# FFN2 of a retention kernel by a seven-product block scheme, in groups of two units

## The chip, the cores and the metric

The kernel runs on one core of one Trainium2 chip. The metric is the device time of one launch in microseconds, median of several runs on that core; the profile shows one such run, whose span is 1.7 to 1.9 us shorter than its time. Executions come in a fast and a slower state.

## The reference, cut to what matters

Retention (causal attention with a decay per head, no softmax) over 8 batches, 8 heads, 576 positions, 64 columns a head, and on its output `x` (4608 x 512) a feed-forward block with a squared Relu:

```python
ret = scale * (q @ k.T) * Dmat            # Dmat: gamma_h ** (i - j) for i >= j, else 0
x = (ret @ v)                             # heads side by side: 4608 x 512
h = x @ w_in                              # FFN1: 512 -> 2048
r = np.maximum(h, 0.0)
g = r * r
out = (g @ w_out).astype(np.float32)      # FFN2: 2048 -> 512
```

## The kernel before

The rows are cut into 36 units of 128. A small list scheduler in Python orders all work: each task has an engine, a key (its place), a duration as planned, the tasks it depends on and the buffers it takes; it is simulated once, and the instructions of each engine are issued in that order. So the order on an engine is fixed when the kernel is built, and an instruction that waits holds up what stands behind it on its engine.

Most units go in groups of 4, so that FFN1's moving operand is 512 wide. ScalarE takes the Relu out of the accumulating bank, VectorE squares it, and FFN2 runs per unit with 16 matmuls of N=512 (`NF` is 16 blocks of the hidden layer, `NP` 4 of the model width `DM` = 512, `P` is 128):

```python
sizes = [1, 1, 2, 2, 2] + [4] * 7
...
nc.tensor.matmul(tile_of["ph", g, fb][:, j, :], lhsT=w_in16[:, m, fi * P:(fi + 1) * P],
                 rhs=tile_of["x", us[0]][:, m, :], start=(m == 0), stop=(m == NP - 1))      # FFN1, L559
...
nc.scalar.activation(out=t, in_=tile_of["ph", g, fb], func=ACTF.Relu)                       # rl, L567
...
nc.vector.tensor_tensor(out=t, in0=rl, in1=rl, op=ALU.mult)                                 # gT, L572
...
nc.tensor.matmul(tile_of["po", u, lo], lhsT=tile_of["g", g, fi // nf][:, fi % nf, s * P:(s + 1) * P],
                 rhs=w_out16[:, fi, lo:hi], start=(fi == 0), stop=(fi == NF - 1))           # FFN2, L589
...
nc.scalar.copy(out=o, in_=tile_of["po", u, lo])                                             # to SBUF, then stored
```

GpSimd feeds the retention part. For each unit it casts k twice and q once from fp32 to fp16 (one input each) and multiplies v with a column of decays; it reads all four from SBUF. In what follows these four are "the casts of a unit". The cast k and q then go through DMA transposes, out of a few staging buffers `kq`.

Of the kernel before, what the change touches and what calls it, by code (L numbers as in the profile page):

```python
# [101 lines left out]
def kernel(  # L102
# [9 lines left out]
    nc = tc.nc  # L112
# [16 lines left out]

    sizes = [1, 1, 2, 2, 2] + [4] * 7  # L130
    assert sum(sizes) == NU
    groups = []
    for n in sizes:
        first = sum(len(g) for g in groups)
        groups.append(list(range(first, first + n)))
    groups[-1][-2:] = groups[-1][:-3:-1]
    group_of = {u: g for g, us in enumerate(groups) for u in us}
# [5 lines left out]
    work = ctx.enter_context(tc.tile_pool(name="work", bufs=3))  # L143
    o_pool = ctx.enter_context(tc.tile_pool(name="o", bufs=3))
    x_pool = ctx.enter_context(tc.tile_pool(name="x", bufs=3))
    st_pool = ctx.enter_context(tc.tile_pool(name="st", bufs=5))
    g_pool = ctx.enter_context(tc.tile_pool(name="g", bufs=32))
    r_pool = ctx.enter_context(tc.tile_pool(name="r", bufs=3))
    ps_ff = ctx.enter_context(tc.tile_pool(name="ps_ff", bufs=3, space=bass.MemoryType.PSUM))
    ps_sc = ctx.enter_context(tc.tile_pool(name="ps_sc", bufs=2, space=bass.MemoryType.PSUM))  # L150
# [46 lines left out]
    for hp in range(NP):  # L197
        nc.scalar.activation(out=gam_f[:, hp, :], in_=iota_f, func=ACTF.Exp, scale=lncol[:, hp:hp + 1])
    gam = {"full": gam_f}
    dec128 = const.tile([P, NP], FP32, name="dec128")  # L200
# [4 lines left out]
    vps = [const.tile([P, NP, 192], FP16, name=f"vp{i}") for i in range(NB)]  # L205
    NT = 3
    kTs = [const.tile([P, NP, 2, P], FP16, name=f"kTb{i}") for i in range(NT)]

# [6 lines left out]

    NK = 3
    kqs = [const.tile([P, 3 * NP, P], FP16, name=f"kq{i}") for i in range(NK)]
# [3 lines left out]
    for t in kqs[1:]:  # L221
# [3 lines left out]
    L = 2 * NF  # L225
    WARM = 48
    XBAR = 8
    FIRST = ["u0", "u1", "u2", "u3", "w0", "w1", "w2", "w3", "w4", "w5", "w6", "w7"]
    sched = Schedule(dict(ff=3, psc=2, psT=1, psS=1, psO=1, ld=5, wst=4, k16=4, q16=2,
                          qT=3, rT=2, x=3, rl=3, o=3, R=5, kqT=3))  # L230
    add = sched.add
# [37 lines left out]
    def make_tail_pool():  # L269
        make_mask("tail")  # L270
        nc.gpsimd.memset(mask["tail"][0:64, 64:128], 0.0)
        iota_pt = tile_of["iota_pt"] = const.tile([P, 1], FP32, name="iota_pt")
        nc.gpsimd.tensor_copy(out=iota_pt[0:64], in_=iota_p[0:64])
        nc.gpsimd.tensor_scalar(out=iota_pt[64:128], in0=iota_p[64:128], scalar1=-64.0, scalar2=None, op0=ALU.add)
        gam_t = gam["tail"] = const.tile([P, NP, P], FP32, name="gam_tail")
        nc.gpsimd.tensor_copy(out=gam_t[:, :, 0:64], in_=gam_f[:, :, 0:64])
        nc.gpsimd.tensor_copy(out=gam_t[:, :, 64:128], in_=gam_f[:, :, 0:64])
    tail_pool = add_gated("POOL", 4, "v", 2.2, make_tail_pool)
# [57 lines left out]
    def add_ret(u):  # L336
        kind, b, c = units[u]
        us = groups[group_of[u]]
        base = (u - len(us)) * L
        early = u < ahead  # L340
# [43 lines left out]
        def ft(i, src):  # L384
            def f():
                if i == 0:
                    tile_of["psk", u] = ps_one.tile([P, 2, NP, P], FP16, name="psT", tag="psT")
                elif early:
                    tile_of["psq", u] = ps_sc.tile([P, 2, NP, P], FP16, name="psTq", tag="psc")
                else:  # L390
                    tile_of["psq", u] = tile_of["psk", u]
                for hp in range(NP):
                    nc.tensor.transpose(tile_of["ps" + src[0], u][:, i, hp, :],  # L393
                                        tile_of[src, u][:, hp * P:(hp + 1) * P], ident)
            return f
# [17 lines left out]
        else:  # L413
            prev = [T["score", u - NT]] if u >= NT else zeroed[u]
            tk = add("PE", base - 17.6, 0.22, ft(0, "k16"), deps=[ck] if early else [ck, cq], acq=("psT",))
            tq = add("PE", base - 17.5, 0.22, ft(1, "q16"), deps=[cq, tk], acq=("psc",) if early else ())
# [5 lines left out]
            if early:  # L422
                sched.free("psT", [e0, e1])
                sched.free("psc", [eq])
            else:
                sched.free("psT", [e0, e1, eq])
            transposed = [e0, e1, eq]
# [8 lines left out]
        if kind == "full":  # L436
# [15 lines left out]
            else:  # L452
                def fr0():
                    tmp = tile_of["tmp", u] = work.tile([P, NP, P], FP32, name="stmp", tag="stmp", bufs=2)
                    nc.vector.tensor_tensor(out=tmp, in0=tile_of["psS", u].rearrange("p n a d -> p n (a d)"),  # L455
# [72 lines left out]
        def fx():  # L528
            if s == 0:
                tile_of["x", us[0]] = x_pool.tile([P, NP, len(us) * P], FP16, name="xT", tag="xT")  # L530
            nc.vector.tensor_tensor(out=tile_of["x", us[0]][:, :, s * P:(s + 1) * P], in0=tile_of["psO", u],  # L531
                                    in1=gam[kind], op=ALU.mult)
        T["x", u] = add("DVE", base + 22.6, 0.7, fx, deps=[outs[-1]] + ([T["x", us[0]]] if s else []),
                        acq=() if s else ("x",))
        sched.free("psO", [T["x", u]])
        T["out", u] = outs[-1]


    T["ff2"] = []

    def add_ff(g):
# [5 lines left out]
        sq = []  # L547
        done = g - 1
        while done >= 0 and sum(4 * len(groups[i]) for i in range(done, g + 1)) <= 32:
            done -= 1  # L550
        before = [T["ff2"][done]] if done >= 0 else []
        for fb in range(NF // nf):
            for j in range(nf):
                def f(fb=fb, j=j):
# [3 lines left out]
                    for m in range(NP):  # L558
                        nc.tensor.matmul(tile_of["ph", g, fb][:, j, :], lhsT=w_in16[:, m, fi * P:(fi + 1) * P],  # L559
                                         rhs=tile_of["x", us[0]][:, m, :], start=(m == 0), stop=(m == NP - 1))  # L560
                f1.append(add("PE", base + (nf * fb + j) * n, 0.01 + 0.2133 * n, f,
                              deps=[T["x", u] for u in us] + before + wcast[(nf * fb + j) // 4] + f1[-1:],
                              acq=("ff",) if j == 0 else ()))
# [4 lines left out]

            def fg(fb=fb):
                t = tile_of["g", g, fb] = g_pool.tile([P, nf, n * P], FP16, name="gT", tag="gT")  # L570
                rl = tile_of["rl", g, fb]
                nc.vector.tensor_tensor(out=t, in0=rl, in1=rl, op=ALU.mult)  # L572
            r = add("ACT", base + 4 * fb + 4, 0.6, fr, deps=[f1[-1]], acq=("rl",))
            sched.free("ff", [r])
            sq.append(add("DVE", base + 4 * fb + 6, 0.45, fg, deps=[r]))
            sched.free("rl", [sq[-1]])
        sched.free("x", [f1[-1]])
        for s, u in enumerate(us):
            kind, b, c = units[u]
            end = base + NF * (n + s + 1)  # L580
            f2 = T["ff2"][-1:] if s == 0 else f2[-1:]

            cuts = [(0, DM)] if u != groups[-1][-1] else [(0, DM // 2), (DM // 2, DM)]
            for ci, (lo, hi) in enumerate(cuts):
                for fi in range(NF):
                    def f(fi=fi, s=s, u=u, lo=lo, hi=hi):
                        if fi == 0:
                            tile_of["po", u, lo] = ps_ff.tile([P, hi - lo], FP32, name="po", tag="ff")
                        nc.tensor.matmul(tile_of["po", u, lo], lhsT=tile_of["g", g, fi // nf][:, fi % nf, s * P:(s + 1) * P],  # L589
                                         rhs=w_out16[:, fi, lo:hi], start=(fi == 0), stop=(fi == NF - 1))  # L590
                    f2.append(add("PE", base + NF * (n + s) + fi / len(cuts) + 8 * ci, 0.0025 + 0.2135 / len(cuts), f,
                                  deps=[sq[fi // nf]] + wcast[4 + fi // 4] + f2[-1:],
                                  acq=("ff",) if fi == 0 else ()))

                def fo(u=u, lo=lo, hi=hi):
                    o = tile_of["o", u, lo] = o_pool.tile([P, hi - lo], FP32, name="o", tag="o")
                    nc.scalar.copy(out=o, in_=tile_of["po", u, lo])  # L597

                def fd(u=u, kind=kind, b=b, c=c, lo=lo, hi=hi):
                    o = tile_of["o", u, lo]  # L600
                    if kind == "full":
                        r0 = b * S + c * P
                        nc.scalar.dma_start(out=out[r0:r0 + P, lo:hi], in_=o)
                    else:
                        for i in range(2):
                            r0 = (b + i) * S + 512
                            nc.scalar.dma_start(out=out[r0:r0 + 64, :], in_=o[i * 64:(i + 1) * 64])
                oc = add("ACT", end + 1, 0.12 + 0.47 / len(cuts), fo, deps=[f2[-1]], acq=("o",))
                sched.free("ff", [oc])
                st = add("ACT", end + 1.1, 0.05, fd, deps=[oc], after=2.5)  # L610
                sched.free("o", [st])
        T["ff2"].append(f2[-1])

# [38 lines left out]
```

## Time and profile before

| | before |
|---|---|
| time, median of 3 runs | 323.06 us (322.87 to 323.6) |
| span of the profiled run | 322.6 us (this run took 324.27) |
| matmuls of FFN1 and FFN2 | 1008 of N=512, 224 of N=256 |
| FFN2 of two units | 32 matmuls of N=512 x 0.2158 = 6.9 us |
| VectorE, ScalarE, GpSimd busy | 57%, 40%, 36% |

The prediction below shows the lines that this rests on. They are to be read so: TensorE issues without a gap from about 72 us on, so the only measure of its work is the distance from one matmul's start to the next one's (0.2158 us at N=512, 0.1090 at N=256, 0.0557 at N=128). From this I work out two numbers of every trace. "Steps" is the sum of these distances over all matmuls, by their widths. A "stall" is what the distance between two consecutive starts has beyond the step of the first. Before has 308.5 us of steps and 7.4 us of stalls, nearly all ahead of 72 us.

### The profile page before, as it was taken

Reading aid. Unit: us, or ns where it says so; the run is one execution under the profiler, and the core shown is the slowest. Engines: PE = TensorE matmul, PEld = TensorE weight load, DVE = VectorE, ACT = ScalarE, POOL = GpSimd, SP = SyncE. Lnnn points to the kernel's source line nnn. Section 1 sums busy time; section 2 is a strip of 40 time slices with the busy share of each in tenths; the row PEclk is TensorE's granted clock in tenths of the full one; section 3 lists DMA queues with packets and bytes.
Section 4 is the critical chain, followed back from the end, with each engine's and each line's share of the span. In section 5 each row is a group of like instructions: output and inputs, shape, how many; then the busy total and the mean of one; then the engine's idle time right before and its main releaser. Section 6 shows DMA issues by size and latency. Waiting matters only on the chain.

```text
span 322.6 us, 5955 instructions
## 1 busy us (share of the span) xinstructions
PE 312.5 (97%) x2304; PEld 182.1 (56%) x2304; DVE 183.9 (57%) x341; ACT 128.8 (40%) x217; POOL 115.7 (36%) x167
## 2 busy tenths in 40 slices
PE   5999989989999999999999999999999999999996
PEld 2679746766855555555555555555555555554444
DVE  3496528676947843863488447833685367523500
ACT  4448843522515511551155115511552155215611
POOL 5724486625535643343347433323334200000000
PEclk9999999999999999999999999999999999999999
DMA  9999999999999999999999987799323802010012
GB/s 169 218 375 385 345 231 235 215 199 216 230 213 214 202 196 266 227 213 242 245 227 228 197 221 165 141 193 209 73 50 83 163 33 51 33 67 33 0 65 69
DMA packets 166061, 57.55 MB, mean 178 GB/s; under 512 B 157200, under 2 KB 157456, under 8 KB 166032
## 3 DMA queue, kind: packets, MB, share of 16 engines
q1 hardware_dynamic: 160640, 47.72, 74.2%
q10 hardware_dynamic: 5392, 9.44, 8.8%
q8 instruction: 18, 0.29, 0.4%
q14 instruction: 11, 0.09, 0.1%
HBM read 36.70 MB, written 9.44 MB: 143 GB/s over the span
## 4 chain that ended last, share of the span: by engine, by line
PE 85%; DMA 7%; DVE 4%; issue 1%; POOL 1%; ACT 1%; POOLq 0%; SPq 0%
PE po L589 36%; PE ph L559 33%; PE psO L512 4%; PE psc L480 4%; PE warm L242 3%; DMA wo<-in_moe_w_out_dram 3%; PE psS L441 2%; DMA kqT<-kq 2%; PE psO L516 2%; DMA out_dram<-o 1%; DVE rT L488 1%; DMA k<-in_k_dram 1%; DVE R L460 1%; DVE stmp L455 1%; PE psT L393 0%
## 5 line engine op out<-in xcount | busy, mean ns | idle before, releaser
L589 PE MATMUL po<-w_out,gT 128*128 128x512 f16 (+1 forms) x592 | 144.5, 373 | 1.0 <-POOL w_out L321 1.0
L559 PE MATMUL ph<-xT,w_in 128*128 128x512 f16 (+2 forms) x768 | 138.0, 326 | 0.0
L567 ACT ACTIVATE rl<-ph 128x512 f16<-128x512 f32 x144 | 85.6, 597 | 58.3 <-PE ph L559 54.4
L559 PEld LDWEIGHTS <-w_in 128*128 128x128 f16 x768 | 66.7, 98 | 42.0
L572 DVE TENSOR_TENSOR gT<-rl 128x512 f16<-128x512 f16 x144 | 71.7, 511 | 28.6 <-ACT rl L567 27.7
L589 PEld LDWEIGHTS <-gT 128*128 128x128 f16 x592 | 55.8, 98 | 45.5 <-issue 1.2
L597 ACT COPY o<-po 128x512 f32<-128x512 f32 (+1 forms) x37 | 21.2, 574 | 115.6 <-PE po L589 101.7
L365 POOL TENSOR_TENSOR vp<-v,vdec_full 128x512 f16<-128x512 f32 x32 | 34.0, 1064 | 38.8 <-PE psO L516 17.4
L488 DVE TENSOR_TENSOR rT<-psc,mask_full 128x512 f16<-128x512 f32 x64 | 41.6, 681 | 4.7 <-PE psc L480 4.4
L531 DVE TENSOR_TENSOR xT<-psO,gam_full 128x512 f16<-128x512 f32 x32 | 22.1, 690 | 34.6 <-PE psO L516 23.0
L512 PEld LDWEIGHTS <-vp 128*128 128x128 f16 x288 | 25.4, 98 | 15.9 <-issue 1.0
L348 POOL CAST kq<-k 128x512 f16<-128x512 f32 x28 | 19.2, 684 | 42.3 <-DMA kqT<-kq 21.4
L512 PE MATMUL psO<-rT,vp 128*128 128x128 f16 x288 | 34.0, 219 | 0.2
L455 DVE TENSOR_TENSOR stmp<-psS,R 128x512 f32<-128x512 f32 x24 | 16.5, 689 | 25.0 <-PE psS L441 24.7
L356 POOL CAST kq<-q 128x512 f16<-128x512 f32 x28 | 19.5, 696 | 28.9 <-DMA kqT<-kq 23.0
L480 PEld LDWEIGHTS <-kqT 128*128 128x128 f16 x224 | 19.3, 98 | 16.0 <-DMA kqT<-kq 2.3
L480 PE MATMUL psc<-kqT 128*128 128x128 f16 x224 | 26.1, 219 | 1.9 <-DMA kqT<-kq 1.9
L352 POOL CAST k<-k 128x512 f16<-128x512 f32 x36 | 23.3, 647 | 8.3 <-PE psS L441 5.6
L460 DVE TENSOR_TENSOR R<-stmp,bdec 128x512 f16<-128x512 f32 x24 | 18.4, 765 | 0.8
L242 PE MATMUL warm<-kq,ident 128*128 128x512 f16 x48 | 15.5, 438 | 3.3 <-DVE kq L218 3.3
L516 PE MATMUL psO<-kqT,R 128*128 128x128 f16 (+1 forms) x104 | 17.9, 211 | 0.0
L441 PEld LDWEIGHTS <-k 128*128 128x128 f16 x128 | 9.8, 98 | 6.2
(63 smaller groups left out, 123.0 us busy)
## 6 DMA issues: line engine op xcount, KB each, us to landing
k<-in_k_dram SPq DMA_DIRECT2D x32, 256.0 KB, 4.8
q<-in_q_dram SPq DMA_DIRECT2D x32, 256.0 KB, 5.0
v<-in_v_dram SPq DMA_DIRECT2D x32, 256.0 KB, 5.0
out_dram<-o ACTq DMA_DIRECT2D x31, 256.0 KB, 3.7
wi<-in_moe_w_in_dram SPq DMA_DIRECT2D x4, 1024.0 KB, 10.5
wo<-in_moe_w_out_dram SPq DMA_DIRECT2D x4, 1024.0 KB, 9.3
out_dram<-o ACTq DMA_DIRECT2D x10, 128.0 KB, 2.4
k<-in_k_dram SPq DMA_DIRECT2D x8, 128.0 KB, 5.0
```

What stands on the lines that cost most here:

```text
L242: nc.tensor.matmul(warm_ps[0], lhsT=ident, rhs=junk, start=True, stop=True)
L352: nc.gpsimd.tensor_copy(out=t, in_=tile_of["k32", u].rearrange("p h d -> p (h d)"))
L365: nc.gpsimd.tensor_tensor(out=vo, in0=tile_of["v32", u].rearrange("p (n a) d -> p n a d", a=2), in1=vdec[kind].rearrange("p (n a o) -> p n ...
L480: nc.tensor.matmul(tile_of["psc", u, half][:, j, a, :], lhsT=k_T(hp, a), rhs=q_T(hp), start=True, stop=True)
L488: nc.vector.tensor_tensor(out=tile_of["rT", u][:, 2 * half:2 * half + 2].rearrange("p n a i -> p (n a) i"), in0=tile_of["psc", u, half].re ...
L512: nc.tensor.matmul(ps[:, hp, :], lhsT=vps[u % NB][:, hp, a * 64:a * 64 + P], rhs=tile_of["rT", u][:, hp, a, :], start=(a == 0), stop=(a == ...
L516: nc.tensor.matmul(ps[:, hp, lo:hi], lhsT=tile_of["R", ru][:, hp, :], rhs=q_T(hp)[:, lo:hi], start=False, stop=(n == len(inter) - 1))
L531: nc.vector.tensor_tensor(out=tile_of["x", us[0]][:, :, s * P:(s + 1) * P], in0=tile_of["psO", u], in1=gam[kind], op=ALU.mult)
L559: nc.tensor.matmul(tile_of["ph", g, fb][:, j, :], lhsT=w_in16[:, m, fi * P:(fi + 1) * P], rhs=tile_of["x", us[0]][:, m, :], start=(m == 0) ...
L567: nc.scalar.activation(out=t, in_=tile_of["ph", g, fb], func=ACTF.Relu)
L572: nc.vector.tensor_tensor(out=t, in0=rl, in1=rl, op=ALU.mult)
L589: nc.tensor.matmul(tile_of["po", u, lo], lhsT=tile_of["g", g, fi // nf][:, fi % nf, s * P:(s + 1) * P], rhs=w_out16[:, fi, lo:hi], start=( ...
```

## The change

The intent is to take matmul columns off TensorE. For two units A and B, FFN2 is a product of a 2x2 block matrix G (rows: units A, B; columns: the halves of the hidden layer) with a 2x2 block matrix W. The change computes it with seven block products in place of eight (Strassen's scheme in its variant with few sums). The sums of W's blocks (`wT`) are made once; the sums of G's blocks (S1 to S4, each in two halves, so eight operations of 128x512 a group) are made on VectorE for every group. Partial sums that two results need are read out of the bank, after which the next product is added to the same bank. All FFN groups become groups of two, five of the eight squares of a group move to ScalarE, and retention runs 20 places further ahead. The diff, cut to its core:

```diff
-    sizes = [1, 1, 2, 2, 2] + [4] * 7
+    sizes = [1, 1] + [2] * 17
...
-    NK = 3                                  # staging buffers of the DMA transposes
+    NK = 2
...
+    EARLY = 20
+    SQ_ACT = (0, 2, 3, 5, 7)
...
-        base = (u - len(us)) * L
+        base = (u - len(us)) * L - EARLY
...
+    t1 = add_wT(0, wB[0, 1], wB[0, 0])      # wB: blocks of w_out; wT: their differences, once
+    t2 = add_wT(1, wB[1, 1], wT[0])
+    t3 = add_wT(2, wB[1, 1], wB[0, 1])
+    t4 = add_wT(3, wB[1, 0], wT[1])
...
+                if on_act:
+                    nc.scalar.activation(out=t, in_=rl, func=ACTF.Square)
+                else:
+                    nc.vector.tensor_tensor(out=t, in0=rl, in1=rl, op=ALU.mult)
...
+    # G(s, i, h): unit s, hidden half i, half h of it;  Sx(k, h): half h of sum k   (VectorE, L665)
+        s3 = add_sum(2, base - 12, G(0, 0, h) - G(1, 0, h), needs low squares)
+        s1 = add_sum(0, base,      G(1, 0, h) + G(1, 1, h), needs all squares)
+        s2 = add_sum(1, base + 1,  Sx(0, h) - G(0, 0, h),   needs s1[h])
+        s4 = add_sum(3, base + 4,  G(0, 1, h) - Sx(1, h),   needs s2[h])     # written short
...
+                    for i in (2 * q, 2 * q + 1):
+                        nc.tensor.matmul(tile_of["pb", g, bank], lhsT=left(i), rhs=right[:, i, :],
+                                         start=(start and i == 0), stop=(i == HF - 1), skip_group_check=not start)
...
+        p1 = product(1, 0, "a", raw(0, 0), wB[0, 0], low, True, True, [])
+        c1 = on_act_copy("p1", "a", 5, [p1])                 # reads the bank, which goes on adding
+        p7 = product(7, 4, "c", summed(2), wT[2], lambda h: [s3[h]], True, True, [])
+        p6 = product(6, 8, "a", summed(1), wT[1], lambda h: [s2[h]], False, True, [c1])
+        c2 = on_act_copy("u2", "a", 13, [p6])
+        p2 = product(2, 12, "b", raw(0, 1), wB[1, 0], high, True, True, [])
+        d11 = on_dve_add(uA, 0, "b", "p1", 17, [p2, c1], ("o",))
+        p5 = product(5, 16, "a", summed(0), wT[0], lambda h: [s1[h]], False, True, [c2])
+        c4 = on_act_copy("u4", "a", 21, [p5])
+        d22 = on_dve_add(uB, 1, "c", "u4", 22, [p7, c4], ("o",))
+        p3 = product(3, 20, "a", summed(3), wB[1, 1], lambda h: [s4[h]], False, True, [c4])
+        p4 = product(4, 24, "c", raw(1, 1), wT[3], high, False, True, [d22])
```

The left operand of product 6 is S2 = S1 - G of A's first half, and S1 needs the last square of the group. So between the last block of FFN1 and the second half of product 6 lies a chain on ScalarE and VectorE: Relu, square, S1, S2. TensorE covers it with retention work, product 1 and product 7. In the views below `gT<-rl` is a square, `gS<-gT` a half of S3 or S1, `gS<-gS,gT` a half of S2, and `gS<-gT,gS` a half of S4.

## The prediction

> **What bounds the kernel now.** I read the page's busy table and slices first, then the chain that ended last, then the costliest groups, and last the order in time of TensorE, VectorE and ScalarE in the steady part.
>
> ```profile
> span 322.6 us, 5955 instructions
> ...
> PE 312.5 (97%) x2304; PEld 182.1 (56%) x2304; DVE 183.9 (57%) x341; ACT 128.8 (40%) x217; POOL 115.7 (36%) x167
> ...
> PE   5999989989999999999999999999999999999996
> ...
> PEclk9999999999999999999999999999999999999999
> ...
> PE 85%; DMA 7%; DVE 4%; issue 1%; POOL 1%; ACT 1%; POOLq 0%; SPq 0%
> ...
> L572 DVE TENSOR_TENSOR gT<-rl 128x512 f16<-128x512 f16 x144 | 71.7, 511 | 28.6 <-ACT rl L567 27.7
> ```
>
> TensorE is busy 97%, and the chain of waits is 85% TensorE. But a busy TensorE need not be a full one, since the ends of matmuls are modelled. So I take starts, not durations, from the chain of waits in order of time (start, us, what):
>
> ```profile
> 81.79 2.18 PE ph L559 x20
> ...
> 291.67 13.81 PE ph L559 x64
> ```
>
> 20 matmuls of N=256 (group of two) step by 2.18/20 = 0.1090 us; 64 of N=512 step by 13.81/64 = 0.2158 us; N=128 steps by 0.0557 (8 scores in 0.45). One group of four units in the steady part, from its first hidden-layer matmul at 128.11 to the next group's at 160.66, lasts 32.55 us. Its work is 64+64 matmuls of N=512 (27.62), about 84 of N=128 (4.68) and 8 of N=64 (0.2): 32.5 us. There is no idle time in it. TensorE is the bound by issue rate itself, from about 72 us on. Idle TensorE exists only before that: 0.98 us on the w_out cast, then 1.41 and 0.47 us on transposed k and q:
>
> ```profile
> 65.11 0.62 PE L480 MATMUL psc<-kqT 128*128 128x128 f16 x8 [1.41 <-DMA kqT<-kq]
> ...
> 70.35 0.29 PE L480 MATMUL psc<-kqT 128*128 128x128 f16 x2 [0.47 <-DMA kqT<-kq]
> ```
>
> Columns taken off TensorE therefore come off the time, as long as VectorE and ScalarE can bear what is put on them. These lines say how fast VectorE is (start, us, operation, count):
>
> ```profile
> 132.27 2.60 DVE L572 TENSOR_TENSOR gT<-rl 128x512 f16<-128x512 f16 x4
> 134.83 0.69 DVE L531 TENSOR_TENSOR xT<-psO,gam_full 128x512 f16<-128x512 f32 x1
> ...
> 262.89 1.22 DVE L572 TENSOR_TENSOR gT<-rl 128x512 f16<-128x512 f16 x3
> ...
> 269.60 0.42 DVE L572 TENSOR_TENSOR gT<-rl 128x512 f16<-128x512 f16 x1
> ```
>
> An fp16 product in SBUF takes 0.42 us alone, but 0.65 each in the run at 132.27, when GpSimd was casting. The mean of all is 0.511. An operation reading PSUM takes 0.69, with a step of about 0.61 when the next one follows at once. ScalarE's Relu takes 0.60, a copy of 128x256 0.37.
>
> **What the Trainium skill says.** "TensorE: Matmul & The Clock Gate", section Back-to-back issue gap, gives N/2.4 + 2.5 ns: 109 for N=256 and 216 for N=512. The trace agrees (109.0, 215.8). So two halves cost 1% more than one whole. The same section's other figure, about 131 ns for N=512 in a stream with weight loads, is contradicted by the 215.8, which has a load per matmul. "VectorE: DVE Perf Modes", The perf-mode tier table: tensor_tensor reaches 2x with 16-bit SBUF operands, 1x with any PSUM operand. 0.42 against 0.69 agrees, so the new sums should be of the fast kind. "SBUF — State Buffer", Who interferes with whom: a VectorE instruction with two SBUF inputs contends with a GpSimd one that reads SBUF. The 0.42 against 0.65 agrees. Every new sum has two SBUF inputs. "PSUM — Partial Sum Buffer", The four PSUM rules: a matmul without the first flag adds to what stands in the bank. Nothing in this trace shows a bank read halfway and then added to; before, each bank is read once after its last matmul.
>
> **The change part by part.** There are 19 groups now: two of 1, seventeen of 2. Fifteen (units 4 to 33) use Strassen; the last is ordinary.
>
> 1. FFN2. Per Strassen group, 32 matmuls of N=512 (6.906 us) become 7 products of 8, 56 of N=256 (6.104): -0.802, times 15 = -12.0 us.
> 2. FFN1. 28 units go from groups of 4 to groups of 2: per four units 64 x 0.2158 = 13.81 becomes 128 x 0.1090 = 13.95: +0.14, times 7 = +1.0 us. Counted the other way from the built order: 1008 matmuls of N=512 and 224 of N=256 become 80 and 1960: 241.9 us becomes 230.9. TensorE's sum: -11.0 us.
> 3. VectorE, per Strassen group: 5 of 8 squares leave for ScalarE (-5 x 0.51); 8 half sums of 128x512 fp16 come (+8 x 0.51 = 4.1) and 3 additions of PSUM and SBUF, 128x256, which I estimate at 0.69 less 256 elements at 0.96 GHz = 0.42 each (1.3). Net +2.8, times 15 = 42 us. Once, 8 sums of weight blocks of 1024 elements, at about 0.7 each: 5.5. VectorE goes from 184 to about 231 of some 313, 74%.
> 4. ScalarE: +5 squares (0.60, as Relu, same width and no second table load in the order), 2 copies of 0.585 become 4 of 0.37: +3.3 per group, 50 in all: 129 becomes 179, 57%.
> 5. GpSimd only loses the tail gamma tile. DMA bytes are unchanged. Retention runs 20 keys, 20/32 of a unit, further ahead of its group; q and k staging buffers fall from 3 to 2.
>
> **The steady period by hand.** Per group TensorE needs 64 x 0.109 + 56 x 0.109 + 2 x 1.27 (retention) = 15.6 us, against 16.3 for two units before. I walk the built order with the durations above, time zero being the end of FFN1's second block. The eighth block ends at 5.8. ScalarE after it: relus 2 to 8 and squares of blocks 3, 4, 6, 8, eleven operations of 0.6 in all counting relu 2, end at about 7.2, 1.45 after the eighth block. TensorE meanwhile has 6 matmuls of retention, product 1 with 6 more (done at +1.55), product 7 (+2.42), then product 6, whose second half comes at +2.85. Product 1's copy out of its bank (0.37) ends at about +2.1; product 6, which adds to that bank, is to start at +2.42: 0.3 to spare. Product 6's second half needs a VectorE chain of 14 operations from the square of the second block (start 0.97) on: 3 squares and 7 sums at a step of 0.435 (0.511 less the overlap of 0.08), two PSUM masks, stmp and R, 2.6 together, and 0.45 for four dependent pairs. That is 7.4, so done at 8.35, or +2.6: 0.25 to spare. With sums at the contended 0.65, six of ten, it would be late by about 1 us. After that come product 2, product 5, the next group's first block, product 3, and product 4; their additions and copies have some 0.3 us or more each. ScalarE's last store issue waits for the last addition and ends 0.4 before the next relu.
>
> So the order fits, with small spare at two places. I take 0.2 us of stalls per group on average, 3 us over 15. The two early waits on transposed k and q should go, as units 8 and 9 are scored later relative to their load (-1.9), but the weight sums load VectorE in 42 to 58 us, where it had 7 us free of 16 (+1). The end is unchanged: last outputs still in two halves; the last group's FFN1 without retention beside it has ScalarE 11 x 0.6 = 6.6 against TensorE's 6.1, hidden because FFN2 needs the last square only 3 us later.
>
> Sum: 323.1 - 11.0 - 1.9 + 1.0 + 3.0 = 314.2; I choose 313.8, since the contention falls when GpSimd ends.
>
> **The rivals.** First, VectorE becomes the bound. For it: 14 us of busy time per 15.6 us period (3 squares, 8 sums, 3 additions, 4 masks, 2 x, 2 stmp, 2 R), strict order on the engine, and contention on ten operations of the critical chain. Against it: busy durations overlap by 0.08 each when operations follow at once, so it needs about 12.2. If it is true, each group stalls 0.8 us or more, the gain is eaten, and the time is 322 or worse. Second, the shared bank: read, wait, add again, three times a group; each round trip is matmul end, semaphore, 0.37 us copy, semaphore. The order puts another product (0.87) between, so it is hidden, unless ScalarE is late: its 7.8 us of FFN1 work barely fits the 7.6 of TensorE's. If exposed at 0.3 us a time, 13 us are lost and the result is within 2%. Third, a supply limit: two staging buffers instead of three for the DMA transposes (4.7 us each, one per 7.8 us). In the kernel before GpSimd waited up to 7.1 us for these buffers without TensorE ever waiting after 71 us; five units of buffering remain, so I give it little. It would show as TensorE waiting for kqT, some us.
>
> **Range and chances.** With no stall at all and the early waits gone: 310.2. With 0.5 us per group: 318. I take 310.5 to 318.5. The limit of 2% is 316.6, which needs stalls of about 0.38 us per group. Faster 0.82, same 0.16, slower 0.02.
>
> **What will show it.** The step of 56 product matmuls near 0.109; TensorE's busy near 301 to 304; VectorE 225 to 235, ScalarE near 179; sums near 0.5 us and 0.42 after GpSimd ends; the period of a Strassen group 15.6 to 15.9. If TensorE waits for gS, VectorE was too slow; if for copies of po, the bank trip is exposed; if for kqT, supply. A step of product matmuls clearly over 0.109, or sums at 1x (0.65 or more alone), would break the prediction.

## The result

| | before | changed kernel |
|---|---|---|
| time, median | 322.97 us (322.87 to 323.6, 4 runs) | 318.92 us (318.02 to 319.73, 4 runs) |
| span of the profiled run | 322.6 us | 317.0 us |
| TensorE: steps + stalls | 308.5 + 7.4 | 297.4 + 12.9 |
| VectorE, ScalarE busy | 183.9, 128.8 us | 226.3, 176.8 us |

The ratio is 0.987, with a 95% interval of 0.984 to 0.990. Ratios here are the mean time of one kernel's fast runs over that of the other's in the same rounds, so they aren't quite the ratios of the medians quoted. A gain of 4 us came where 9 were predicted. The result was computed right.

The page of the changed kernel (span; TensorE in 40 slices; the chain that ended last, by engine):

```profile
span 317.0 us, 7736 instructions
...
PE   5999979999999999999999999999999998999995
...
PE 67%; DVE 14%; DMA 8%; SPq 5%; issue 3%; ACT 2%; POOL 1%; ACTq 0%; DVEq 0%
```

In the chain TensorE falls from 85% to 67% and VectorE rises from 4% to 14%: the end is now in part set by VectorE, although TensorE's slices look as full as before. The waits of the changed kernel say where (engine, line, waited for: us in total, times, longest):

```profile
POOL kq L350 <- DMA kqT<-kq: 61.7, 16, 8.8
...
DVE gS L665 <- ACT gT L612: 4.6, 16, 0.4
...
PE po L687 <- DVE gS L665: 5.1, 7, 1.1
```

TensorE waits 7 times for a half sum `gS`, 5.1 us by the view. Counted from starts it is 7.0 us ahead of the products that read half sums, all of it product 6's second half waiting for S2, in 9 of 15 groups. Waits for copies of the bank don't appear: product 1's copy ends 2.12 us after FFN1's last block, and product 6 starts at 2.42. The groups of VectorE operations (us busy, mean ns):

```profile
L614 DVE TENSOR_TENSOR gT<-rl 128x512 f16<-128x512 f16 x64 | 31.7, 495 | 25.9 <-ACT rl L602 25.5
L665 DVE TENSOR_TENSOR gS<-gT 128x512 f16<-128x512 f16 x60 | 29.4, 489 | 5.8 <-ACT gT L612 4.6
...
L665 DVE TENSOR_TENSOR gS<-gT,gS 128x512 f16<-128x512 f16 x30 | 17.6, 586 | 0.0
L665 DVE TENSOR_TENSOR gS<-gS,gT 128x512 f16<-128x512 f16 x30 | 16.4, 546 | 1.0
L710 DVE TENSOR_TENSOR o<-po,u 128x256 f32<-128x256 f32 x30 | 12.6, 419 | 22.9 <-PE po L687 22.1 <-ACT u L700 0.8
```

These means are close to what was predicted (0.511 for a sum, 0.42 for an addition out of PSUM). The means hide two kinds of groups. First a stalled one. VectorE in order of time (start, us, operation), FFN1's last block ending at 162.91:

```profile
163.12 0.42 DVE L665 TENSOR_TENSOR gS<-gS,gT 128x512 f16<-128x512 f16 x1
163.46 0.83 DVE L614 TENSOR_TENSOR gT<-rl 128x512 f16<-128x512 f16 x1
164.21 0.83 DVE L665 TENSOR_TENSOR gS<-gT,gS 128x512 f16<-128x512 f16 x1
164.96 0.83 DVE L665 TENSOR_TENSOR gS<-gT 128x512 f16<-128x512 f16 x1
165.82 1.15 DVE L665 TENSOR_TENSOR gS<-gS,gT 128x512 f16<-128x512 f16 x1
```

GpSimd in the same stretch of the same trace:

```profile
163.14 0.87 POOL L350 CAST kq<-k 128x512 f16<-128x512 f32 x1 [7.11 <-issue]
163.96 0.81 POOL L354 CAST k<-k 128x512 f16<-128x512 f32 x1
164.71 0.80 POOL L358 CAST kq<-q 128x512 f16<-128x512 f32 x1
165.48 1.21 POOL L367 TENSOR_TENSOR vp<-v,vdec_full 128x512 f16<-128x512 f32 x1
```

TensorE, at the first and second half of product 6:

```profile
164.45 1.47 PE L687 MATMUL po<-wT,gS 128*128 128x256 f16 x12
167.02 0.61 PE L687 MATMUL po<-wT,gS 128*128 128x256 f16 x4 [1.10 <-DVE gS L665]
```

While TensorE stands there, product 2 stands behind product 6, though it reads only squares, and the last of these was done at 164.37.

The two engines take turns. Each VectorE operation ends 0.28 us after a cast ends, and the next one 0.27 us or so after the next cast. A sum that takes 0.42 alone takes 0.83, the cast beside it 0.80 in place of the 0.61 of most casts in this trace, and both go on at one pair per 0.75 us, where VectorE alone goes on at 0.34. Beside the multiply of v a sum takes 1.15. S2's second half ends at 166.97, where an undisturbed group (2.38 us after FFN1) would have had it at 165.29, and TensorE stands for 1.3 us (1.10 by the view, which counts from a modelled end).

An undisturbed VectorE stretch in the group before (FFN1's last block ends at 147.34) has its casts 0.8 us later:

```profile
147.89 0.42 DVE L614 TENSOR_TENSOR gT<-rl 128x512 f16<-128x512 f16 x1
148.22 0.42 DVE L665 TENSOR_TENSOR gS<-gT,gS 128x512 f16<-128x512 f16 x1
148.83 0.56 DVE L665 TENSOR_TENSOR gS<-gT 128x512 f16<-128x512 f16 x1 [0.19 <-ACT gT L612]
149.42 0.72 DVE L665 TENSOR_TENSOR gS<-gS,gT 128x512 f16<-128x512 f16 x1
150.06 0.68 DVE L534 TENSOR_TENSOR xT<-psO,gam_full 128x512 f16<-128x512 f32 x1
```

GpSimd there:

```profile
148.34 0.78 POOL L350 CAST kq<-k 128x512 f16<-128x512 f32 x1 [6.47 <-DMA kqT<-kq]
149.06 0.81 POOL L354 CAST k<-k 128x512 f16<-128x512 f32 x1
149.81 0.80 POOL L358 CAST kq<-q 128x512 f16<-128x512 f32 x1
150.58 1.04 POOL L367 TENSOR_TENSOR vp<-v,vdec_full 128x512 f16<-128x512 f32 x1
```

Only two chain operations are touched, S2 ends 2.80 us after FFN1, and TensorE, which comes to it at 2.86, doesn't wait. The `xT` at 150.06, which has only one input in SBUF, takes its usual 0.68 beside two of the casts.

So the theory after reading the trace (theory 1): GpSimd's reading casts and VectorE's two-input operations take turns at one place, and a group stalls when a unit's casts fall on the chain. Its rivals: VectorE simply has too much to do in the chain (theory 2, the prediction's first rival), or the order of work on VectorE puts other operations ahead of S2 (theory 3).

### The profile page after: what moved, and what is told of

Read it like the earlier page. It is cut to its first block, busy times and chain, and to the rows that moved or that the text cites. A ratio compares the mean times of both kernels' runs of the same rounds, so it can differ in the third digit from the quotient of the medians.

```text
span 317.0 us, 7736 instructions
## 1 busy us (share of the span) xinstructions
PE 302.6 (95%) x3112; PEld 260.3 (82%) x3112; DVE 226.3 (71%) x433; ACT 176.8 (56%) x327; POOL 118.9 (38%) x163
## 4 chain that ended last, share of the span: by engine, by line
PE 67%; DVE 14%; DMA 8%; SPq 5%; issue 3%; ACT 2%; POOL 1%; ACTq 0%; DVEq 0%
PE ph L594 28%; PE po L687 23%; DVE gS L665 8%; PE po L635 6%; DMA wi<-in_moe_w_in_dram 4%; PE psc L482 4%; SPq L298 4%; DMA wo<-in_moe_w_out_dram 3%; PE psO L514 3%; DVE gT L614 3%; DVE rT L490 2%; PE psS L443 2%; PE psO L518 1%; ACT rl L602 1%; ACT gT L612 1%
## 5 line engine op out<-in xcount | busy, mean ns | idle before, releaser
L594 PE MATMUL ph<-xT,w_in 128*128 128x256 f16 (+1 forms) x1216 | 140.2, 267 | 0.5 <-POOL w_in L323 0.5
L594 PEld LDWEIGHTS <-w_in 128*128 128x128 f16 x1216 | 109.9, 98 | 11.8 <-POOL w_in L323 0.7
L350 POOL CAST kq<-k 128x512 f16<-128x512 f32 x28 | 18.9, 674 | 99.1 <-DMA kqT<-kq 61.7
L687 PEld LDWEIGHTS <-gS 128*128 128x128 f16 x480 | 44.9, 98 | 12.6 <-DVE gS L665 7.9
L687 PE MATMUL po<-wT,gS 128*128 128x256 f16 x360 | 48.9, 273 | 5.4 <-DVE gS L665 5.1
L612 ACT ACTIVATE gT<-rl 128x512 f16<-128x512 f16 x80 | 50.4, 630 | 2.6
L614 DVE TENSOR_TENSOR gT<-rl 128x512 f16<-128x512 f16 x64 | 31.7, 495 | 25.9 <-ACT rl L602 25.5
L700 ACT COPY u<-po 128x256 f32<-128x256 f32 x30 | 11.2, 373 | 53.9 <-PE po L687 53.9
L687 PE MATMUL po<-w_out,gT 128*128 128x256 f16 x240 | 37.6, 273 | 0.0
L687 PEld LDWEIGHTS <-gT 128*128 128x128 f16 x360 | 32.3, 98 | 2.7 <-issue 0.2
L665 DVE TENSOR_TENSOR gS<-gT 128x512 f16<-128x512 f16 x60 | 29.4, 489 | 5.8 <-ACT gT L612 4.6
L635 PE MATMUL po<-w_out,gT 128*128 128x512 f16 (+1 forms) x112 | 23.5, 349 | 1.8 <-POOL w_out L323 1.8
```

The costliest lines, as they stand in the source:

```text
L612: nc.scalar.activation(out=t, in_=rl, func=ACTF.Square)
L635: nc.tensor.matmul(tile_of["po", u, lo], lhsT=tile_of["g", g][:, fi, s * P:(s + 1) * P], rhs=w_out16[:, fi, lo:hi], start=(fi == 0), stop= ...
L665: nc.vector.tensor_tensor(out=Sx(k, h), in0=in0(h), in1=in1(h), op=op)
L687: nc.tensor.matmul(tile_of["pb", g, bank], lhsT=left(i), rhs=right[:, i, :], start=(start and i == 0), stop=(i == HF - 1), skip_group_chec ...
```

## The experiments

All are timed against the kernel before on the same chip. The last column takes the stalls ahead of the half-sum products out of the profiled run's own time.

| run | median us | ratio [95%] | these stalls, us | profiled time less these stalls |
|---|---|---|---|---|
| changed kernel | 318.92 | 0.987 [0.984, 0.990] | 7.0 | 311.7 |
| changed kernel again | 317.94 | 0.983 [0.980, 0.985] | 6.4 | 311.8 |
| pool_gated | 312.32 | 0.968 [0.965, 0.970] | 0.2 | 311.8 |
| pool_writes (wrong result) | 313.07 | 0.969 [0.966, 0.972] | 0.1 | 313.7 |
| pool_collide | 329.70 | 1.021 [1.018, 1.025] | 18.8 | 311.1 |
| s2_first | 315.92 | 0.979 [0.977, 0.981] | 4.8 | 311.7 |
| both | 313.18 | 0.970 [0.968, 0.972] | 0.8 | 312.0 |
| gated_sq_dve | 313.80 | 0.972 [0.970, 0.974] | 1.1 | 312.9 |
| early0 | 317.66 | 0.985 [0.982, 0.987] | 6.2 | 312.6 |
| gated_early0 | 313.38 | 0.970 [0.968, 0.972] | 1.0 | 313.0 |
| nk3 | 316.48 | 0.979 [0.976, 0.982] | 4.3 | 311.3 |
| no_strassen | 323.55 | 1.002 [1.000, 1.005] | none | 323.6 |
| before again (one look) | 322.78 | | none | 322.8 |

The eleven runs with the seven products differ by 17 us in their medians, and without this one stall their profiled runs lie within 2.6 us of each other.

### Is it GpSimd? Casts held back until S2 is done (pool_gated)

One element of the finished second half of S2 is copied by GpSimd, and the casts of the units that come next are put behind that copy:

```diff
+        def fgate():
+            t = tile_of["gate", g] = work.tile([P, 1], FP16, name="gate", tag="gate", bufs=2)
+            nc.gpsimd.tensor_copy(out=t, in_=Sx(1, 1)[:, HF // 2 - 1, P - 1:P])
+        gt = add("POOL", -6 * L, 0.1, fgate, deps=[s2[1]])
+        for w in (uA + 6, uB + 6):
+            for x in T.get(("burst", w), []):      # tasks: k's two casts, q's cast, v's product
+                sched.need(x, gt)
```

> Right result. In each Strassen group GpSimd may begin the casts of two later units only after it has read one element of the last half of sum S2, so its casts cannot fall on the VectorE chain that ends with S2. Theory A (the lost gain is TensorE waiting for S2 because GpSimd reads and two-input VectorE operations take turns): the stalls ahead of product 6's second half, 7.0 us in the changed kernel's trace, fall below 1.5 us, sums in the chain take 0.42 to 0.45 us, time about 312.5 to 314. Theory B (VectorE has simply too much work per group, whoever else runs): stalls stay at 6 us or more, time 318 to 319. Theory C (supply: casts delayed by the gate come too late): stalls move to TensorE waiting for transposed k and q or for vp, time 319 or more.

It ran in 312.32 us, 6.6 below the changed kernel, with a right result. Page (span, TensorE in slices, chain):

```profile
span 310.3 us, 7730 instructions
...
PE   5989979999999999999999999999999999999995
...
PE 85%; DMA 8%; SPq 5%; POOL 1%; issue 0%; ACT 0%
```

VectorE is gone from the chain. Its operations in order of time, one group (FFN1's last block ends at 160.51):

```profile
161.06 0.42 DVE L615 TENSOR_TENSOR gT<-rl 128x512 f16<-128x512 f16 x1
161.40 0.42 DVE L666 TENSOR_TENSOR gS<-gT,gS 128x512 f16<-128x512 f16 x1
162.00 0.42 DVE L666 TENSOR_TENSOR gS<-gT 128x512 f16<-128x512 f16 x1 [0.19 <-ACT gT L613]
162.46 0.43 DVE L666 TENSOR_TENSOR gS<-gS,gT 128x512 f16<-128x512 f16 x1
...
165.17 1.38 DVE L463 TENSOR_TENSOR R<-stmp,bdec 128x512 f16<-128x512 f32 x1
```

The chain now runs at 0.42. The turn-taking isn't gone: it fell on the retention state `R`, another operation with two SBUF inputs (mean 0.88 here, 0.78 in the changed kernel), where it costs little: in the five groups in which `R` took 1.37 to 1.38 us, and in no other, product 4 started 0.16 us late (it waits for an addition that VectorE does after `R`), 0.8 us in the whole run. Steady periods are 15.56 to 15.94 us; in the changed kernel they reach 17.05.

### Is it the reading, or the time at which GpSimd works? (pool_writes)

From unit 8 on, GpSimd does five memsets per unit in place of the casts and the multiply, so it writes no less than before and reads nothing (it is busy for 101.2 us, against 118.9). The result is wrong.

```diff
+            if xbar:
+                nc.gpsimd.memset(
+                    kq[:, 0:2 * NP].rearrange("p (n a) (b d) -> p n (a b) d", a=2, d=64)[:, :, 0:4:3, :], 0.125)
+                nc.gpsimd.memset(t, 0.125)
+                return
...
+                nc.gpsimd.memset(kq[:, 2 * NP:].rearrange("p n c -> p (n c)"), 0.125)
...
+                nc.gpsimd.memset(vo, 0.125)
+                nc.gpsimd.memset(vo, 0.125)
```

> Wrong result on purpose. From unit 8 on, GpSimd writes constants of the same shapes (5 memsets per unit in place of 3 casts and a product) and reads nothing. If it is GpSimd's reading that slows the two-input VectorE operations, the sums take 0.42 us throughout although GpSimd is as busy as before, stalls ahead of product 6 fall below 1 us, time 312 to 314. If any GpSimd work slows them, sums stay near 0.49 to 0.59 mean and time 317 to 319.

313.07 us; one of its four runs was slow (319.53 at a granted clock of 0.989) and isn't in the ratio. The median of the three fast ones is 312.37. The same group as the stalled one above (FFN1's last block ends at 162.41), GpSimd:

```profile
162.29 0.52 POOL L351 MEMSET kq<- 128x512 f16 x1 [3.57 <-DMA kqT<-kq]
162.76 0.52 POOL L353 MEMSET k<- 128x512 f16 x1
163.22 0.52 POOL L359 MEMSET kq<- 128x512 f16 x1
163.69 0.52 POOL L368 MEMSET vp<- 128x512 f16 x1
```

VectorE in the same stretch:

```profile
162.96 0.42 DVE L618 TENSOR_TENSOR gT<-rl 128x512 f16<-128x512 f16 x1
163.29 0.42 DVE L669 TENSOR_TENSOR gS<-gT,gS 128x512 f16<-128x512 f16 x1
163.90 0.43 DVE L669 TENSOR_TENSOR gS<-gT 128x512 f16<-128x512 f16 x1 [0.19 <-ACT gT L616]
164.36 0.42 DVE L669 TENSOR_TENSOR gS<-gS,gT 128x512 f16<-128x512 f16 x1
```

GpSimd is as near as can be in time, and VectorE isn't touched. So it is neither GpSimd's being at work nor its writing; what the casts and the product have beyond a memset is that they read (and convert or multiply what they read; no run parts these two). The Trainium skill says this in "SBUF — State Buffer", Who interferes with whom (a VectorE instruction with two SBUF inputs contends with a GpSimd instruction that reads SBUF, not with one that only writes), and both halves of the sentence are seen here: 0.83 beside reads, 0.42 beside writes. In its fast runs it is as fast as pool_gated (312.37 and 312.32). The profiled run is the slowest of the three, and has an early wait of 1.9 us for a transposed k and q.

### Casts put on the chain on purpose (pool_collide)

The same gate, reading S3, which is done about 0.95 us ahead of FFN1's end:

```diff
-            nc.gpsimd.tensor_copy(out=t, in_=Sx(1, 1)[:, HF // 2 - 1, P - 1:P])
-        gt = add("POOL", -6 * L, 0.1, fgate, deps=[s2[1]])
+            nc.gpsimd.tensor_copy(out=t, in_=Sx(2, 1)[:, HF // 2 - 1, P - 1:P])
+        gt = add("POOL", -6 * L, 0.1, fgate, deps=[s3[1]])
```

> Right result. The same gate read as in the gated kernel, but on the last half of sum S3, which is done about 0.95 us before the end of FFN1: GpSimd's casts then begin just ahead of the S1 and S2 chain in all 13 groups that have later units, not in some. Theory A: each of those groups shows the stall of 0.85 to 1.0 us that the changed kernel shows where its casts began at -1.3 to -0.9 us, so stalls ahead of product 6 of 11 to 13 us, time 322 to 325, the whole gain gone. Rival: the gate itself gained (GpSimd's casts in pairs, less waiting on its buffers): then it gains wherever it stands, and the time stays at 312 to 314.

329.70 us, 17.4 slower than with the gate that reads S2, and 4.7 above the range expected. The waits, and two groups of VectorE operations of it:

```profile
PE po L696 <- DVE gS L666: 16.5, 13, 1.8
```

```profile
L666 DVE TENSOR_TENSOR gS<-gT,gS 128x512 f16<-128x512 f16 x30 | 29.8, 992 | 0.0
...
L666 DVE TENSOR_TENSOR gS<-gS,gT 128x512 f16<-128x512 f16 x30 | 19.6, 654 | 1.0
```

The S4 sums, of which the first half stands in VectorE's order ahead of the second halves of S1 and S2, take 0.99 us on average, against 0.47 in pool_gated, and the S2 sums 0.65 against 0.43. The groups stall by up to 1.9 us. The expectation was too low because two units' casts now follow each other: while the first unit's four are being worked off the chain falls behind, and then it meets the second unit's (in the group whose FFN1 ends at 149.47 the first four run from 148.83 to 152.12 and the next begin at 152.19; S2 ends at 153.90, 4.4 us after FFN1).

### Is it the load, or the order, on VectorE? (s2_first, both, gated_sq_dve)

s2_first puts S1 and S2 ahead of S4 and of the next `xT`, which takes operations out of the chain (theory 3). "both" does this and has the gate.

```diff
-        s4 = add_sum(..., lambda h: [s2[h]])
+        s4 = add_sum(..., lambda h: [s2[h], s2[1]])
+        if uB + 2 < NU:
+            sched.need(T["x", uB + 2], s2[1])
```

> Right result. Only VectorE's order: both halves of S1 and S2 go ahead of S4 and of the evacuation xT, which product 6 does not need. Theory A or B (the chain that ends with S2 is too long): one contended sum (0.83 us) less ahead of S2, so each stalled group gets 0.5 to 0.8 us back, stalls 7.0 to about 2, time 313.5 to 315.5. If the late product is not due to the chain's length but to ScalarE's last square: no change, 318 to 319.

> Right result. The gate after S2 together with VectorE's order S1, S2 ahead of S4 and xT. With no contention left on the chain the order has nothing to win: the stalls of product 6 are already 0.2 us in the gated kernel. Expected the same as the gated kernel within 0.3%, 311.5 to 313.5; a time below 311 would say that the chain still costs something that the stalls do not show.

s2_first ran in 315.92 us, about halfway and 0.4 above the range expected: 4.8 us of stalls remain where about 2 were expected, because a sum beside the multiply of v is as slow in the new order. VectorE and GpSimd in one group of it:

```profile
196.45 0.64 DVE L665 TENSOR_TENSOR gS<-gT 128x512 f16<-128x512 f16 x1
197.13 1.15 DVE L665 TENSOR_TENSOR gS<-gS,gT 128x512 f16<-128x512 f16 x1
```

```profile
196.02 0.80 POOL L358 CAST kq<-q 128x512 f16<-128x512 f32 x1
196.78 1.21 POOL L367 TENSOR_TENSOR vp<-v,vdec_full 128x512 f16<-128x512 f32 x1
```

"both" took 313.18 us, 0.9 more than the gate alone. A shorter chain is worth nothing once the casts are off it, and putting the sums first makes others wait: TensorE's stalls ahead of the retention products that read masked scores (`psO<-rT,vp`) are 1.6 us in place of 0.1.

The sharpest test of theory 2 loads VectorE more: the gate, with all eight squares back on VectorE.

```diff
-    SQ_ACT = (0, 2, 3, 5, 7)
+    SQ_ACT = ()
```

> The gated version, with all eight squares of a group back on VectorE (none on ScalarE); the kernel's own scheduler orders the work anew. VectorE then gets five more operations of 0.42 us per group, a step of 0.34 each, so about 1.7 us more in a period of 15.6; ScalarE loses 5 x 0.63. Theory A (what cost the change its time is GpSimd's turn-taking, not VectorE's load): the load still fits, the group's last square even ends sooner, since ScalarE does only relus; stalls ahead of the products from half sums stay under 0.3 us per group and the time is 311 to 315. Theory B (rival 1 as predicted: VectorE as such is too full for its chain): 1.7 us more in the chain shows as 0.8 us or more of stall per group, and the time is 322 or more.

313.80 us. Its page (busy times; chain):

```profile
PE 302.7 (97%) x3112; PEld 261.1 (84%) x3112; DVE 257.7 (83%) x513; ACT 133.7 (43%) x247; POOL 120.3 (39%) x178
...
PE 83%; DVE 7%; DMA 5%; issue 2%; ACT 1%; POOL 1%; POOLq 0%; SPq 0%; DVEq 0%
```

VectorE is busy for 257.7 us, 31 more than in the changed kernel and 83% of the span, and the kernel is 5 us faster than the changed one. Theory 2 falls. The scheduler ordered the work anew in this run, so it doesn't price the move of the squares by itself; it shows that the load fits.

### The other parts of the change (no_strassen, early0, gated_early0, nk3)

```diff
-    STRASSEN = 3
+    STRASSEN = 99        # no_strassen: groups of 2 and retention ahead stay; all squares on VectorE
```

> Right result. Strassen is off: FFN2 with 32 matmuls of N=512 per group again and all squares on VectorE; groups of 2, the early retention, the smaller buffers and the (now unused) 8 weight sums stay. By the matmul steps TensorE's sum is 297.4 + 12.0 = 309.5 us, against 308.5 before. If the rest of the change costs only those 1.0 us of FFN1: time 322.5 to 324.5. If the groups of 2 or the earlier retention bring waits of their own, more, 326 or above; if they save the early waits, 321.5.

323.55 us; TensorE's steps are 309.5 us, 1.0 above before, and 12.0 above the changed kernel. So the groups of two cost 1.0 us of TensorE and the seven products save 12.0, both as in the prediction. Between this run and the changed kernel only 4.6 of the 12 reach the time, between it and pool_gated 11.2.

```diff
-    EARLY = 20
+    EARLY = 0            # early0; gated_early0 is this with the gate
```

> Right result. The changed kernel with its retention not brought forward (20 keys later, as before the change). If the bringing forward was needed to keep TensorE fed (masks, evacuations and transposed k and q in time), TensorE waits for scores or states in every group, time 321 or more. If it is not needed, what is left is where GpSimd's casts fall: stalls of 3 to 9 us as in the changed kernel, time 315 to 321.

> The gated version with retention not further ahead (20 keys taken back). Without the gate this was 1.3 us faster than the change as it stands (317.66 against 318.92), with stalls ahead of the half-sum products of 6.2 instead of 7.0 us. Theory A (that difference is only where the casts happened to fall): with the gate it is gone, 311.8 to 313.2, within 0.3% of the gated 312.3. Theory B (running retention less far ahead is worth something by itself): 311.3 or less. Theory C (the distance is needed for supply once casts are held back): TensorE waits on transposed k and q, 314 or more.

early0 317.66, gated_early0 313.38. Running less far ahead is thus not shown to be worth anything of its own: it was 1.3 us faster without the gate (the changed kernel's own two medians differ by 1.0), and with it 1.1 us slower than pool_gated, with intervals of the ratios that overlap (0.2 above what was expected if only the places of the casts counted; its profiled run has 1.5 us in which TensorE waits for the multiply of v, which speaks for some need of the distance). TensorE has no wait for transposed k and q in early0 either, so the distance isn't what removed them.

The staging buffers fell from 3 to 2, and in the changed kernel GpSimd waits 61.7 us for them, 16 times: the end of a DMA transpose decides when the casts start. nk3 gives the third back, for one output buffer:

```diff
-    NK = 2
+    NK = 3
-    o_pool = ctx.enter_context(tc.tile_pool(name="o", bufs=4))
+    o_pool = ctx.enter_context(tc.tile_pool(name="o", bufs=3))
```

> The change with three staging buffers of transposed input instead of two, as the kernel before had (paid for with one output buffer). Theory A (the two buffers only decide when GpSimd may cast, so a third moves the casts to other places, without keeping them off the chain): stalls ahead of the half-sum products of 3 to 10 us, time 315 to 322. Theory B (the cut from three buffers to two is what set the casts onto the chain; with three they would follow the data and stay clear): stalls under 2 us, 312 to 314.

316.48 us with 4.3 us of stalls. The buffers move the casts about, and here less often onto the chain; they don't keep them off. This run changes an output buffer too, so the 1.5 us to the changed kernel run beside it aren't put down to one of the two.

### The changed kernel and the kernel before, once more (after_again, before_again)

> The change as it stands, once more. Theory (stalls come from where GpSimd's casts happen to fall on the chain of half sums): the median is again 318 to 320, the profile has 6 to 8 us of stalls ahead of the half-sum products, again in the groups whose casts begin between 2.4 us before and 0.5 us after the end of FFN1. If another set of groups is hit but the rule of the place holds, that also agrees; stalls in groups without casts there would speak against it.

> The kernel before, unchanged, for a second trace: how much the waits of its first 72 us (2.2 us on transposed k and q, 1.2 on the w_out cast in the first trace) vary from one execution to the next. Steady part without stalls as before. If the 2.2 us are typical they are there again, span 322 to 323; if they were of that execution, span about 321.

The changed kernel again took 317.94 us (0.06 below the range expected) with 6.4 us of stalls. The rule as I had put it, by the start of the casts, wasn't good enough: one group stalled 1.0 us with casts that began 1.2 us after FFN1. A better one counts how long GpSimd's casts lie in the stretch from 2.0 us ahead of the end of FFN1's last block to 2.4 us after it, which is where the chain lies. It was made after seeing these groups, so it describes them and isn't a test. Over the 30 groups of both profiled runs of the changed kernel:

| casts in that stretch | groups | stall ahead of product 6's second half, mean us (range) |
|---|---|---|
| under 0.9 us | 8 | 0.04 (0 to 0.28) |
| 0.9 to 2.2 us | 10 | 0.27 (0 to 1.00) |
| over 2.2 us | 12 | 0.86 (0.57 to 1.27) |

The one group with a stall and no casts in the stretch (0.28) had been delayed by casts further ahead: a square of 0.88 and a half sum of 1.15 us beside them, some 4 us before FFN1's end, left its S3 1.2 us later than in an undisturbed group.

The kernel before again took 322.78 us, and TensorE's stalls were 5.9 us, 1.5 less than in the run that the prediction started from. The waits on transposed k and q were 1.2 us in it, against 2.2, so part of them was of that one execution.

## Why the prediction was wrong

It predicted 313.8 (310.5 to 318.5); 318.92 came. By its own steps:

- **TensorE's sum, -11.0 us:** right to 0.1 (308.5 to 297.4). Also right were N=256 at 0.109 a product matmul, +1.0 for groups of two, and -12.0 for the products (no_strassen).
- **VectorE about 231, ScalarE 179:** 226.3 and 176.8. An addition out of PSUM, estimated at 0.42, took 0.419; a square on ScalarE 0.63 against 0.60.
- **Stalls, "0.2 us of stalls per group on average, 3 us over 15":** this step failed. It was 0.47 per group, 7.0 in all (6.4 in the second run), 4 of the 5.1 us by which the prediction missed. The chain was timed with the mean duration (a step of 0.435) and found to have 0.25 us to spare. Undisturbed it was better than that: S2 ends 2.38 us after FFN1 and TensorE comes to it at 2.85. But a mean over all operations isn't what a chain meets. Where a unit's casts fall on it, each operation takes 0.83 to 1.15, not the 0.65 that the prediction named as contended (that figure was the mean of one line of the view with x4: taken one by one in the trace of before, the four are 0.74 and 1.26 beside GpSimd's work, then 0.41 and 0.41 after it). One unit's casts delay four chain operations by 1.7 us in the group shown, 0.5 of it is spare, and 1.2 remain. 12 of 30 groups were hit in full. The prediction had worked out that contended sums would make product 6 about 1 us late, not far from the mean of 0.86 in these groups; what it lacked was how often the casts would fall there.
- **Early waits, -1.9 + 1.0:** the waits on transposed k and q did go, but against the second run of before (stalls 5.9) the changed kernel's stalls outside the half-sum products are also 5.9 (12.9 - 7.0; in its second run 12.3 - 6.4). Against the first run of before (7.4) they are 1.5 less. So, counted from the median, little or nothing was gained: the gain was read from a profiled run that was itself 1.2 us above the median from which it was then subtracted. That is up to 0.9 us of the miss.
- **313.8 in place of the 314.2 of its sum:** 0.4 of the miss, for contention that ends with GpSimd's work. It does end (no stall in the last two groups), but those are two of 15.
- **First rival, VectorE becomes the bound:** the place was right and the reason wrong. It was put as load, 14 us in a period of 15.6; gated_sq_dve has more load and no such stall.
- **Second rival, the shared bank:** product 1's copy ended 0.3 us ahead of its use, as worked out by hand. TensorE's stalls ahead of product 4, which waits for an addition that reads its bank, are 0.2 us in all (0.8 in pool_gated, from `R` as told above).
- **Third, supply:** TensorE's waits for transposed k and q are 0.03 us. But two buffers let the DMA transposes decide when the casts start, which the prediction didn't connect with contention.

With the casts off the chain the change gives 312.32 us, 10.3 less than before (medians), inside the range predicted.

What stays open: whether the remaining early waits (about 3.5 us in pool_gated, TensorE waiting for the casts of w_in and w_out) can be removed; no run tried it.

## What to carry to other kernels

When a change puts a chain of two-input VectorE operations between two matmuls, don't time it with a mean duration: look at what GpSimd reads during it, and, at these shapes (128x512), plan for a turn of 0.75 us per operation in place of 0.34 if it reads, and for up to 1.15 us beside a two-input multiply. A cheap dependency (a one-element copy of the chain's last output) keeps GpSimd's reads off the chain, here for 6.6 us of 319. And subtract a gain from the same run in which it was read, not from a median of others.

## What the Trainium skill lacked or had wrong

- "SBUF — State Buffer", Who interferes with whom: right on who contends, as above. Its summary (Rules for kernel authors) says that the second one to issue "fully blocks" until the first finishes. In the trace, back-to-back operations take strict turns, one of each per 0.75 us, where one after the other would take 0.34 + 0.55 = 0.89 us by their undisturbed steps, so by these figures a part of each overlaps. The page gives no durations for such a pair; 0.42 becomes 0.83 beside a cast and about 1.15 beside a two-input multiply, and the cast's 0.61 becomes 0.80.
- "TensorE: Matmul & The Clock Gate", Back-to-back issue gap: about 131 ns for N=512 in a stream of weight loads and matmuls isn't reached here. The N/2.4 + 2.5 given beside it for an isolated matmul is what the streams show: 215.8 ns for N=512 and 109.0 for N=256.
- "PSUM — Partial Sum Buffer", The four PSUM rules: it says that a partial sum may be read in the middle of an accumulation, without saying what this costs. All runs with seven products that kept their data were right, with four such reads a group; a read of 128x256 took 0.37 us on ScalarE, and with one other product or one block of FFN1 (8 matmuls of N=256, 0.87 us) between, TensorE didn't wait for it.
